# A fused RWKV-6 attention and SwiGLU kernel: all steps of its hand-ordered schedule put into a new order

## The chip, the core and the metric

The kernel runs on one core of a Trainium2 chip. The core has five engines, each with a queue of its own that it works off in order: TensorE (PE in the profile; its weight loads are shown apart as PEld), VectorE (DVE), ScalarE (ACT), GpSimd (POOL) and SyncE (SP), which here only starts transfers. The metric is the device time of one execution in microseconds (us).

## The reference

Attention with a decaying state per head (4 batches, 8 heads, 768 tokens, head dimension 48), and on its output, laid out as 3072 rows of 384, an RMS norm and a SwiGLU feed-forward with 1536 hidden units:

```python
for t in range(S):
    cur = np.einsum('bhd,bhe->bhde', u[None] * kt, vt)
    y[:, :, t] = np.einsum('bhd,bhde->bhe', rt, state + cur)
    state = wt[:, :, :, None] * state + np.einsum('bhd,bhe->bhde', kt, vt)
...
x = np.ascontiguousarray(attn_out.transpose(0, 2, 1, 3)).reshape(B * S, H * D)
xn = x / np.sqrt(np.mean(x * x, axis=-1, keepdims=True) + 1e-06) * rms_g
g = xn @ w_gate
return (g * (1.0 / (1.0 + np.exp(-g))) * (xn @ w_val)) @ w_out
```

## The kernel before

The 768 tokens are cut into six blocks of 128, n = 0 to 5, for each batch j = 0 to 3. Within a block the recurrence is worked out with matrices: the logarithms of w are summed over time by matmuls, r and k are scaled by the exponentials of these sums, their products (masked to the past) give the part within the block, and a state per head carries the rest to the next block. Blocks 0 and 1 of a batch are done together as a pair, with their rows interleaved, so the first steps take 256 tokens of a batch. The four batches of a block make 512 rows for the feed-forward: 12 units of 128 hidden columns for the gate and 12 for the value, then the product with w_out for each 128 rows. The first such group is cut in halves of 256 rows.

The program is a list of some 1010 steps, one string, in which a step is a function name and two numbers. In most names the numbers are block and batch; `gate_mm.3.10` is block 3, unit 10. A loop at the end calls them in that order:

```python
for step in ORDER.split():
    fn, n, j = step.split(".")
    fns[fn](int(n), int(j))
```

Each function issues a handful of instructions, so the string sets the order in which each engine and each DMA queue gets its work; nothing reorders it later. The steps that the text below speaks of:

- `load_r`, `load_k`, `load_v`, `load_w`: 384 KB each on SP's queue into the stage tiles; `load_gv.g.h`: a third of the gate (h = 0, tiles wg_sb0, wg_sb4, wg_sb8) or value weights (h = 1, wv_sb0, 4, 8) on POOL's queue; `load_wo`: a third of w_out, there too.
- `ln` (ACT), `pcs_mm` or `cs_mm` (PE, sums over time), `cs_add` (DVE), `exp_r` and `exp_k` (ACT), `r_mul` (DVE: r times its factor, tile rk), `k_mul` (DVE or POOL).
- `rk_pe` and `rk_tr`: scaled r and k transposed, in the pair by PE and a copy on ACT, later by DMA transposes on SP's queue (tile rkT).
- `pq_mm` (pair) or `q_mm`: products of r and k on PE; `pmask_e`, `pmask_o`: four masks for each batch on DVE (tile qts); `sta_mm`, `sta_cp`: the state halfway through the pair; `st_mm`, `st_new`: the state at the end of a block; `w_tot`: the decay over a whole block.
- `bonus_mul` (POOL, two products, tile ruk), `bonus_sum` (DVE, tile diag), `bonus_v` (POOL, tile ydiag): the term with u; `cast_v`: v to bf16.
- `y_mm` (PE) and `x_add` (DVE, tile xbs): the attention output; `xd_mm`: in place of one x_add, a matmul with an f32 identity that adds ydiag in PSUM.
- `x_sq`, `x_rstd` (on ACT or POOL), `xn_mul`, `xn_pe`, `xn_out` (tile xnt): the norm and its transpose.
- `pgate`, `pval`, `psilu`, `ph` for the first group's halves, `gate_mm`, `val_mm`, `silu`, `h_mul` for the others (tile ht holds the hidden units); `o_mm`, `o_out`, `out_dma`: the last product and the output. `warm`: fillers for PE, two matmuls of zeros.

PSUM has three rings of banks, two for sums and gates, two for sums and values, four for everything else (ps_a, ps_b, ps_q in the names). Which engine does a step in which block is set by short lists of block and batch such as `K_POOL` and `CAST_ACT`.

Of the kernel before, what the change touches and what calls it, by code (L numbers as in the profile page):

```python
# [26 lines left out]
exp_k.1.0 u_mm.0.0 warm.4.2 load_k.0.0 k_mul.1.0 k_mul.0.0 rk_pe.0.0 rk_tr.0.0 u_cp.0.0 bonus_mul.1.0 bonus_sum.1.0
load_v.0.0 load_w.0.2 load_w.0.1 rk_pe.1.0 warm.0.2 warm.1.2 warm.2.2 warm.3.2 warm.6.2 rk_tr.1.0 pq_mm.0.0 cast_v.0.0
pmask_e.0.0 w_tot.0.0 pq_mm.1.0 pmask_e.1.0 bonus_mul.0.0 ln.0.1 pcs_mm.1.1 pcs_mm.2.1 pmask_o.0.0 ln.0.2 sta_mm.0.0
pcs_mm.0.1 exp_r.1.1 exp_k.1.1 load_r.0.1 r_mul.1.1 exp_k.0.1 exp_r.0.1 load_k.0.1 k_mul.0.1 pmask_o.1.0 pcs_mm.0.2  # L30
pcs_mm.1.2 exp_r.1.2 exp_r.0.2 k_mul.1.1 w_tot.0.1 r_mul.0.1 rk_pe.1.1 rk_tr.1.1 w_tot.0.2 sta_cp.0.0 bonus_v.1.0
load_gv.0.0 gain_mm.0.0 rk_pe.0.1 rk_tr.0.1 y_mm.0.0 load_gv.0.1 pcs_mm.2.2 exp_k.1.2 load_v.0.1 gain_cp.0.0
bonus_sum.0.0 pq_mm.1.1 xd_mm.1.0 load_r.0.2 load_w.0.3 r_mul.1.2 r_mul.0.2 bonus_v.0.0 cast_v.0.1 x_add.0.0
pmask_o.1.1 pmask_e.1.1 bonus_mul.0.1 bonus_mul.1.1 pq_mm.0.1 pmask_e.0.1 ln.0.3 pcs_mm.0.3 sta_mm.0.1 warm.5.2
load_gv.2.0 load_k.0.2 k_mul.1.2 load_gv.2.1 bonus_sum.0.1 pmask_o.0.1 bonus_v.0.1 sta_cp.0.1 x_sq.0.0 x_sq.1.0
exp_k.0.2 k_mul.0.2 x_rstd.0.0 xn_mul.1.0 rk_pe.1.2 pcs_mm.1.3 exp_r.0.3 xn_pe.1.0 xn_out.1.0 pcs_mm.2.3 xn_mul.0.0
rk_tr.1.2 y_mm.0.1 bonus_sum.1.1 w_tot.0.3 xn_pe.0.0 xn_out.0.0 exp_r.1.3 exp_k.0.3 exp_k.1.3 load_r.0.3 x_add.0.1
rk_pe.0.2 warm.7.2 rk_tr.0.2 bonus_v.1.1 r_mul.0.3 x_add.1.1 st_mm.0.1 load_k.0.3 pval.1.0 x_sq.0.1 load_gv.1.0
load_gv.1.1 x_sq.1.1 x_rstd.0.1 k_mul.1.3 st_new.0.1 r_mul.1.3 pgate.1.0 k_mul.0.3 bonus_mul.1.3 load_v.0.2 psilu.1.0
pq_mm.1.2 pq_mm.0.2 pmask_e.1.2 pmask_o.0.2 pgate.0.0 pval.0.0 pmask_o.1.2 st_mm.0.0 st_new.0.0 pmask_e.0.2 rk_pe.1.3  # L40
pgate.5.0 xn_mul.0.1 psilu.0.0 ph.0.0 xn_mul.1.1 bonus_mul.0.3 rk_pe.0.3 rk_tr.0.3 psilu.5.0 bonus_mul.0.2 ph.1.0
pgate.4.0 xn_pe.1.1 xn_out.1.1 load_wo.1.0 xn_pe.0.1 xn_out.0.1 rk_tr.1.3 psilu.4.0 pval.5.0 pval.4.0 pgate.1.1 ph.5.0
psilu.1.1 pq_mm.1.3 pq_mm.0.3 pval.0.1 pgate.0.1 psilu.0.1 ph.4.0 pmask_o.0.3 cast_v.0.2 ph.0.1 bonus_sum.0.2
load_wo.2.0 bonus_mul.1.2 load_wo.0.0 bonus_sum.1.3 pgate.3.0 psilu.3.0 pval.1.1 ph.1.1 bonus_v.0.2 load_v.0.3
cast_v.0.3 pgate.2.0 pval.3.0 pgate.2.1 psilu.2.1 pval.2.0 pmask_o.1.3 bonus_sum.0.3 pmask_e.1.3 sta_mm.0.2 sta_cp.0.2
sta_mm.0.3 psilu.2.0 ph.2.0 load_w.2.0 ln.2.1 ph.3.0 bonus_sum.1.2 bonus_v.1.2 pgate.4.1 pmask_e.0.3 sta_cp.0.3 ln.2.0
psilu.4.1 pgate.5.1 psilu.5.1 pval.2.1 y_mm.0.2 x_add.1.2 x_sq.1.2 bonus_v.1.3 x_add.0.2 ph.2.1 y_mm.0.3 x_sq.0.2
x_rstd.0.2 pgate.3.1 psilu.3.1 pval.3.1 xn_mul.1.2 cs_mm.2.0 cs_add.2.0 ph.3.1 exp_r.2.0 bonus_v.0.3 cs_mm.2.1
cs_add.2.1 exp_k.2.1 x_add.0.3 xn_mul.0.2 st_mm.0.2 o_mm.0.1 exp_k.2.0 load_k.2.0 load_r.2.0 k_mul.2.0 load_w.2.2
x_add.1.3 r_mul.2.0 st_new.0.2 x_sq.1.3 exp_r.2.1 w_tot.2.1 x_sq.0.3 x_rstd.0.3 xn_pe.1.2 k_mul.2.1 bonus_mul.2.1  # L50
pval.5.1 o_mm.0.0 o_out.0.0 pval.4.1 xn_pe.0.2 bonus_mul.2.0 xn_mul.1.3 ph.4.1 ph.5.1 w_tot.2.0 o_out.0.1 o_mm.0.3
r_mul.2.1 xn_out.1.2 xn_out.0.2 ln.2.2 cs_mm.2.2 cs_add.2.2 xn_mul.0.3 ln.2.3 out_dma.0.1 load_w.3.0 load_r.2.2
o_out.0.3 exp_r.2.2 xn_pe.0.3 ln.3.0 load_k.2.2 cs_mm.2.3 xn_pe.1.3 rk_tr.2.1 cs_add.2.3 exp_r.2.3 st_mm.0.3 o_mm.0.2
exp_k.2.3 xn_out.0.3 exp_k.2.2 ln.3.1 xn_out.1.3 val_mm.1.5 rk_tr.2.0 w_tot.2.2 k_mul.2.2 r_mul.2.2 bonus_mul.2.2
w_tot.2.3 bonus_sum.2.0 r_mul.2.3 gate_mm.1.5 silu.1.5 h_mul.1.5 gate_mm.1.1 st_new.0.3 o_out.0.2 silu.1.1 out_dma.0.2
val_mm.1.7 k_mul.2.3 load_v.2.0 bonus_sum.2.1 load_v.2.2 bonus_v.2.1 rk_tr.2.2 gate_mm.1.7 silu.1.7 bonus_mul.2.3
cast_v.2.2 h_mul.1.7 bonus_v.2.0 cast_v.2.0 val_mm.1.1 h_mul.1.1 gate_mm.1.2 silu.1.2 gate_mm.1.4 q_mm.2.0 gate_mm.1.3
q_copy_o.2.1 out_dma.0.3 silu.1.4 q_mask_o.2.1 q_copy_o.2.0 q_mask_e.2.0 q_mask_e.2.1 silu.1.3 val_mm.1.2 h_mul.1.2
val_mm.1.6 gate_mm.1.6 cast_v.2.1 q_mask_o.2.0 st_mm.2.2 st_new.2.2 out_dma.0.0 silu.1.6 val_mm.1.4 h_mul.1.4
gate_mm.1.0 rk_tr.2.3 bonus_sum.2.2 q_mm.2.2 q_copy_o.2.2 h_mul.1.6 silu.1.0 gate_mm.1.10 silu.1.10 val_mm.1.0  # L60
y_mm.2.0 q_mask_o.2.2 bonus_v.2.2 h_mul.1.0 load_r.3.0 load_k.3.0 q_copy_o.2.3 q_mask_e.2.2 gate_mm.1.9 silu.1.9
x_add.2.0 x_sq.2.0 bonus_mul.3.1 bonus_sum.2.3 y_mm.2.1 x_add.2.1 x_sq.2.1 q_mask_e.2.3 val_mm.1.9 h_mul.1.9
q_mask_o.2.3 x_rstd.2.0 x_rstd.2.1 val_mm.1.10 gate_mm.1.11 h_mul.1.10 gate_mm.1.8 y_mm.2.2 x_add.2.2 silu.1.8
xn_mul.2.0 xn_mul.2.1 cast_v.2.3 bonus_mul.3.0 val_mm.1.3 h_mul.1.3 load_k.3.2 x_sq.2.2 st_mm.2.0 cs_mm.3.1 st_new.2.0
silu.1.11 val_mm.1.8 load_w.3.2 ln.3.3 h_mul.1.8 y_mm.2.3 val_mm.1.11 h_mul.1.11 xn_pe.2.0 load_v.3.0 cast_v.3.0
cs_mm.3.0 cs_add.3.0 exp_k.3.0 x_rstd.2.2 xn_mul.2.2 cast_v.3.1 bonus_v.2.3 cs_add.3.1 bonus_sum.3.0 bonus_v.3.0
xn_out.2.0 exp_r.3.0 w_tot.3.0 ln.3.2 o_mm.1.0 exp_k.3.1 k_mul.3.1 k_mul.3.0 exp_r.3.1 x_add.2.3 r_mul.3.0 load_r.3.2
o_out.1.0 x_sq.2.3 x_rstd.2.3 o_mm.1.1 w_tot.3.1 cs_mm.3.2 r_mul.3.1 cs_add.3.2 exp_k.3.2 xn_pe.2.1 st_mm.2.3
st_new.2.3 xn_out.2.1 load_w.4.0 load_w.4.2 o_mm.1.2 o_out.1.1 ln.4.0 load_v.3.2 load_v.4.0 bonus_mul.3.3 rk_tr.3.0
cs_mm.3.3 rk_tr.3.1 xn_mul.2.3 ln.4.1 exp_r.3.2 xn_pe.2.2 xn_out.2.2 cs_add.3.3 out_dma.1.0 xn_pe.2.3 r_mul.3.2  # L70
exp_k.3.3 w_tot.3.2 xn_out.2.3 cast_v.4.1 k_mul.3.2 bonus_sum.3.1 o_out.1.2 load_w.5.2 o_mm.1.3 st_mm.2.1 exp_r.3.3
w_tot.3.3 st_mm.3.0 st_new.3.0 r_mul.3.3 rk_tr.3.2 ln.4.2 val_mm.2.0 st_new.2.1 gate_mm.2.3 silu.2.3 k_mul.3.3
rk_tr.3.3 o_out.1.3 load_k.4.2 load_r.4.0 val_mm.2.3 h_mul.2.3 gate_mm.2.1 silu.2.1 bonus_mul.3.2 gate_mm.2.0 silu.2.0
q_mm.3.0 q_mask_e.3.0 q_copy_o.3.0 q_mask_e.3.1 gate_mm.2.7 gate_mm.2.2 silu.2.2 st_mm.3.1 cast_v.3.3 q_mask_o.3.0
bonus_v.3.1 load_r.4.2 h_mul.2.0 y_mm.3.0 silu.2.7 out_dma.1.2 q_copy_o.3.1 q_mask_o.3.1 val_mm.2.7 gate_mm.2.11
val_mm.2.1 x_add.3.0 x_sq.3.0 x_rstd.3.0 out_dma.1.3 st_new.3.1 h_mul.2.7 bonus_sum.3.3 cast_v.4.0 q_mm.3.2
q_copy_o.3.3 h_mul.2.1 q_mask_e.3.3 cast_v.3.2 q_mask_o.3.3 bonus_v.3.3 load_k.5.2 bonus_mul.4.3 silu.2.11 val_mm.2.11
q_mask_e.3.2 gate_mm.2.6 h_mul.2.11 y_mm.3.1 st_mm.3.3 gate_mm.2.5 val_mm.2.2 st_new.3.3 val_mm.2.6 load_k.4.0
h_mul.2.2 q_copy_o.3.2 q_mask_o.3.2 silu.2.5 xn_mul.3.0 st_mm.3.2 load_w.5.0 y_mm.3.3 silu.2.6 x_add.3.1 h_mul.2.6
x_sq.3.1 gate_mm.2.4 silu.2.4 x_add.3.3 x_sq.3.3 bonus_sum.4.3 val_mm.2.10 gate_mm.2.10 silu.2.10 h_mul.2.10  # L80
val_mm.2.5 gate_mm.2.8 x_rstd.3.1 xn_mul.3.1 gate_mm.2.9 h_mul.2.5 load_v.4.2 x_rstd.3.3 xn_mul.3.3 silu.2.8
bonus_sum.3.2 val_mm.2.4 h_mul.2.4 val_mm.2.8 silu.2.9 y_mm.3.2 st_new.3.2 h_mul.2.8 bonus_mul.4.2 xn_pe.3.3 ln.5.0
out_dma.1.1 load_k.5.0 ln.4.3 val_mm.2.9 h_mul.2.9 xn_out.3.3 bonus_mul.4.1 bonus_v.3.2 cs_mm.4.1 cs_mm.4.0 cs_add.4.0
exp_k.4.0 cs_add.4.1 exp_r.4.1 xn_pe.3.0 xn_out.3.0 load_r.5.2 r_mul.4.1 x_add.3.2 exp_k.4.1 k_mul.4.1 exp_r.4.0
# [742 lines left out]
```

## Time and profile before

| | |
|---|---|
| median of 3 executions | 201.58 us (199.26 to 391.27) |
| profiled execution, its own time | 200.24 us |
| its span | 198.5 us |
| PE, PEld busy | 190.4, 122.2 us |
| DVE, ACT, POOL busy | 145.4, 137.8, 122.8 us |
| DMA | 32.44 MB, mean 163 GB/s |
| granted TensorE clock | 1.0 |

The times from the trace are against the span; 1.74 us lie around it. One of the three executions took 391.27 us, the other two are within 1.2% of one another, and the profiled one lies between these. Busy time is a sum of durations, and a matmul's duration in the trace is longer than the time after which the next one starts, so PE at 96% is partly overlap.

### The profile page before, as it was taken

The numbers are of one execution on the slowest core, as the hardware profiler recorded it, in microseconds if no ns is written. First come the engines' busy times: TensorE is split into PE (matmuls) and PEld (weight loads), VectorE is DVE, ScalarE is ACT, GpSimd is POOL, SyncE is SP. The second block draws the span as 40 slices with busy tenths as digits, with TensorE's granted clock in tenths as the row PEclk, the third lists the DMA queues.
The fourth block names the chain that finished last, engine by engine and source line by source line (L and its number), as shares of the span: only waits on it lengthen the run. The fifth ranks groups of instructions, "written<-read, shape, count | busy, mean of one in ns | idle before, by whom it ended". The sixth has DMA issues, their size and how long they took to land.

```text
span 198.5 us, 5008 instructions
## 1 busy us (share of the span) xinstructions
PE 190.4 (96%) x1932; PEld 122.2 (62%) x1948; DVE 145.4 (73%) x291; ACT 137.8 (69%) x274; POOL 122.8 (62%) x168
## 2 busy tenths in 40 slices
...
PEclk9999999999999999999999999999999999999999
...
GB/s 167 325 323 235 258 221 207 229 214 178 209 146 226 245 202 226 221 210 196 243 207 215 244 146 145 43 40 99 140 122 133 2 25 139 40 0 40 122 59 99
DMA packets 109377, 32.44 MB, mean 163 GB/s; under 512 B 103461, under 2 KB 108969, under 8 KB 109353
## 3 DMA queue, kind: packets, MB, share of 16 engines
...
q0 software_dynamic: 2832, 3.54, 10.2%
...
q14 instruction: 10, 0.07, 0.1%
...
## 4 chain that ended last, share of the span: by engine, by line
PE 65%; DMA 14%; POOL 7%; DVE 6%; SPq 4%; issue 2%; ACT 1%; DVEq 0%; POOLq 0%
PE ps_bu L712 9%; PE ps_au L712 8%; PE ps_av L712 8%; PE ps_qx L769 7%; PE ps_bv L712 7%; DMA wv_sb<-in_moe_w_val_dram 5%; PE ps_qu L769 5%; SPq L259 4%; DMA stage_r<-in_r_dram 3%; DMA stage_v<-in_v_dram 3%; PE ps_qz L769 3%; PE ps_qv L769 3%; DMA stage_w<-in_w_dram 2%; POOL ruk L494 2%; POOL ruk L493 2%
## 5 line engine op out<-in xcount | busy, mean ns | idle before, releaser
L769 PEld LDWEIGHTS <-ht 128*128 128x128 bf16 x300 | 28.4, 98 | 17.0 <-DVE ht L755 0.4
L235 ACT ACTIVATE sg<-ps_au 128x512 bf16<-128x512 f32 x36 | 21.5, 597 | 14.1 <-PE ps_au L712 11.1
L755 DVE TENSOR_TENSOR ht<-ps_bu,sg 128x512 bf16<-128x512 f32 x31 | 21.3, 686 | 12.5 <-ACT sg L235 6.2
L712 PEld LDWEIGHTS <-wv_sb 128*128 128x128 bf16 x180 | 19.4, 114 | 16.9 <-issue 1.6
L235 ACT ACTIVATE sg<-ps_av 128x512 bf16<-128x512 f32 x36 | 21.5, 597 | 11.9 <-PE ps_av L712 8.4
L712 PEld LDWEIGHTS <-wg_sb 128*128 128x128 bf16 x180 | 19.1, 114 | 16.6 <-DVE rk L481 0.8
L493 POOL TENSOR_TENSOR ruk<-stage_r,stage_k 128x384 f32<-128x384 f32 x24 | 24.0, 1000 | 7.0 <-DMA stage_r<-in_r_dram 3.7
L487 POOL TENSOR_TENSOR rk<-stage_k,ek 128x384 bf16<-128x384 f32 x20 | 19.9, 1004 | 10.4 <-ACT ek L235 6.4
L712 PE MATMUL ps_bu<-xnt,wv_sb 128*128 128x512 bf16 x88 | 24.6, 379 | 1.2 <-DVE ht L755 0.8
L494 POOL TENSOR_TENSOR ruk<-ruk,u_bc 128x384 f32<-128x384 f32 x24 | 23.9, 998 | 1.9
L712 PE MATMUL ps_av<-xnt,wg_sb 128*128 128x512 bf16 x89 | 24.9, 380 | 0.2
L755 DVE TENSOR_TENSOR ht<-ps_bv,sg 128x512 bf16<-128x512 f32 x29 | 19.9, 685 | 6.7 <-ACT sg L235 3.0
L712 PE MATMUL ps_au<-xnt,wg_sb 128*128 128x512 bf16 x85 | 23.5, 381 | 0.3
L712 PE MATMUL ps_bv<-xnt,wv_sb 128*128 128x512 bf16 x82 | 23.0, 380 | 0.2
L503 POOL TENSOR_TENSOR ydiag<-stage_v,diag 128x384 f32<-128x384 f32 x24 | 19.7, 830 | 4.5 <-DVE diag L498 4.3
L668 POOL TENSOR_TENSOR rstd<-rstd,mhalf 128x1 f32<-128x1 f32 (+1 forms) x18 | 10.0, 561 | 12.4 <-ACT junk L654 12.4
L769 PE MATMUL ps_qu<-wo_sb,ht 128*128 128x384 bf16 x96 | 16.9, 326 | 0.0
L233 ACT ACT_TABLE_LOAD x12 | 15.4, 1283 | 1.9 <-PEq L811 1.7
L654 ACT ACTIVATE junk<-xbs 128x385 bf16<-128x385 f32 (+1 forms) x23 | 12.2, 529 | 5.8 <-DVE xbs L637 5.7
L672 ACT ACTIVATE xn<-xbs,rstd 128x384 bf16<-128x384 f32 x23 | 13.6, 608 | 3.2 <-POOL rstd L668 3.2
L498 DVE TENSOR_REDUCE diag<-ruk 128x8 f32<-128x384 f32 x24 | 13.0, 544 | 3.7 <-POOL ruk L494 3.7
L769 PE MATMUL ps_qx<-wo_sb,ht 128*128 128x384 bf16 (+1 forms) x96 | 15.0, 306 | 0.0
...
## 6 DMA issues: line engine op xcount, KB each, us to landing
stage_w<-in_w_dram SPq DMA_DIRECT2D x12, 384.0 KB, 5.6
stage_r<-in_r_dram SPq DMA_DIRECT2D x12, 384.0 KB, 6.3
stage_k<-in_k_dram SPq DMA_DIRECT2D x12, 384.0 KB, 6.0
stage_v<-in_v_dram SPq DMA_DIRECT2D x12, 384.0 KB, 5.2
...
wg_sb<-in_moe_w_gate_dram POOLq DMA_DIRECT2D x3, 384.0 KB, 8.0
wv_sb<-in_moe_w_val_dram POOLq DMA_DIRECT2D x3, 384.0 KB, 9.8
```

The costliest lines, as they stand in the source:

```text
L233: nc.scalar.preload_act_table_set(table_name)
L235: return nc.scalar.activation(**kw).ins
L487: eng.tensor_tensor(out=rk[:, n % 2, j, 1, :, 0:D], in0=inp["k", n, j], in1=bank["ek", n, j][:, 0:DM].rearrange("p (h d) -> p h d", h=H), ...
L493: nc.gpsimd.tensor_tensor(out=ruk[n, j], in0=inp["r", n, j], in1=inp["k", n, j], op=ALU.mult)
L494: nc.gpsimd.tensor_tensor(out=ruk[n, j], in0=ruk[n, j], in1=u_bc, op=ALU.mult)
L498: nc.vector.tensor_reduce(out=diag[n, j].rearrange("p h o -> p (h o)"), in_=ruk[n, j], axis=mybir.AxisListType.X, op=ALU.add)
L503: nc.gpsimd.tensor_tensor(out=ydiag[n, j], in0=inp["v", n, j], in1=diag[n, j].to_broadcast([128, H, D]), op=ALU.mult)
L654: nc.scalar.activation(out=junk[:, 0:DM + own], in_=xbuf[n, j] if own else xb[n, j], func=AF.Square, accum_out=rstd[key][:, 0, i:i + 1])
L672: nc.scalar.activation(out=xn, in_=xb[n, j], func=AF.Copy, scale=rstd[0, j][:, 1, n:n + 1] if n in PAIR else rstd[n, j][:, 1, 0:1])
L712: nc.tensor.matmul(ps, lhsT=units(ws, c, f), rhs=xnt[n][:, c, :], start=(c == 0), stop=(c == KC - 1))
L755: nc.vector.tensor_tensor(out=ht[n][:, f, :], in0=bank.pop(("v", n, f)), in1=bank.pop(("sg", n, f)), op=ALU.mult)
L769: nc.tensor.matmul(ps[:, cols], lhsT=ht[n][:, f, b * L:(b + 1) * L], rhs=wo_sb[:, f, cols], start=(f == 0), stop=(f == FC - 1))
```

## The change

The string is new from its start to `y_mm.4.3 gate_mm.3.0`, some seven tenths of it; the rest is as before. With it go these changes in who does what:

- `xd_mm.1.0` is gone; `x_add.1.0` on DVE takes its place, and the f32 identity is no longer made.
- `pcs_mm.2.2`, an addition on DVE before, is two matmuls as in the other batches.
- `cast_v` of batches 1 and 2 goes from ACT to POOL, that of batch 0 from POOL to ACT.
- `k_mul` of 0.0, 0.3 and 1.3 goes from POOL to DVE, that of 0.2 from DVE to POOL (with K_POOL go the buffers of `exp_k`).
- `x_rstd.0.1` goes from ACT to POOL.
- One filler step fewer (seven); the causal mask mask_le has a tile of its own rather than a part of xbs.

New branches in `pq_mm`, `pmask` and `y_mm`, for batches whose pair is not cut in halves, are not taken: every batch has a `sta_mm` step and so is in SPLIT.

```diff
 ORDER = """
-load_w.0.0 ln.0.0 pcs_mm.1.0 exp_r.1.0 exp_k.0.0 load_r.0.0 r_mul.1.0 pcs_mm.0.0 exp_r.0.0 r_mul.0.0 pcs_mm.2.0
...
+load_w.0.0 ln.0.0 pcs_mm.1.0 pcs_mm.2.0 exp_k.1.0 load_k.0.0 k_mul.1.0 u_mm.0.0 exp_r.1.0 exp_k.0.0 u_cp.0.0
...
-    CAST_ACT = sel("01 02 03")
+    CAST_ACT = sel("00 03")
-    K_POOL = sel("00 03 11 13 20 21 22 23 30 31 32 33 40 41 42 43 50 51 52 53")
+    K_POOL = sel("02 11 20 21 22 23 30 31 32 33 40 41 42 43 50 51 52 53")
-    X_PE = sel("10")
+    X_PE = sel("")
-    PCS_ADD = sel("22")
+    PCS_ADD = sel("")
+    ODD_COPY = sel("")
-    RSTD_ACT = sel("00 01")
+    RSTD_ACT = sel("00")
+    SPLIT = {int(x.split(".")[2]) for x in ORDER.split() if x.startswith("sta_mm")}
...
-    mask_le = xbs[:, 2, 0:64].bitcast(BF16)
+    mask_le = const.tile([128, 128], BF16)
...
-    ident_f = const.tile([128, 128], FP32)
-    nc.gpsimd.tensor_copy(out=ident_f, in_=ident)
+    if X_PE:
+        ident_f = const.tile([128, 128], FP32)
+        nc.gpsimd.tensor_copy(out=ident_f, in_=ident)
```

DVE in the front, before: from the sum for the bonus of batch 1 (diag) to the state halfway through the pair of batch 1 (st, sta_cp), which y_mm.0.1 reads. rk rows are r_mul and k_mul, qts rows masks, xbs rows x_add.

```order
L498 TENSOR_REDUCE diag_472<-ruk_291 128x8
L481 TENSOR_TENSOR rk_150<-stage_r_72,ps_bu_356 128x8x48
L481 TENSOR_TENSOR rk_150<-stage_r_72,ps_av_342 128x8x48
L637 TENSOR_TENSOR xbs_80<-ps_qu_392,ydiag_498 128x384
L549 TENSOR_TENSOR qts_492<-ps_qv_475,mask_q_76 128x512
L549 TENSOR_TENSOR qts_492<-ps_qx_474,mask_q_76 128x512
L549 TENSOR_TENSOR qts_529<-ps_qu_511,mask_q_76 128x512
L487 TENSOR_TENSOR rk_150<-stage_k_73,ps_au_467 128x8x48
L498 TENSOR_REDUCE diag_567<-ruk_505 128x8
L549 TENSOR_TENSOR qts_529<-ps_qv_512,mask_q_76 128x512
L568 TENSOR_TENSOR st_153<-ps_qx_543,half_of_138 128x384
```

The same engine and place in the change:

```order
L480 TENSOR_TENSOR wcol_493<-ps_av_340,half_of_139 128x8
L485 TENSOR_TENSOR rk_151<-stage_r_72,ps_av_340 128x8x48
L485 TENSOR_TENSOR rk_151<-stage_r_72,ps_bv_358 128x8x48
L663 TENSOR_TENSOR xbs_80<-ps_qv_418,ydiag_330 128x384
L663 TENSOR_TENSOR xbs_80<-ps_qx_419,ydiag_332 128x384
L587 TENSOR_TENSOR st_154<-ps_qv_525,half_of_139 128x384
L491 TENSOR_TENSOR rk_151<-stage_k_73,ps_au_354 128x8x48
L502 TENSOR_REDUCE diag_555<-ruk_360 128x8
L561 TENSOR_TENSOR qts_514<-ps_qz_497,mask_q_76 128x512
L561 TENSOR_TENSOR qts_587<-ps_qx_569,mask_q_76 128x512
L561 TENSOR_TENSOR qts_587<-ps_qv_570,mask_q_76 128x512
L561 TENSOR_TENSOR qts_514<-ps_qu_496,mask_q_76 128x512
```

The two r_mul of batch 2 (stage_r) stay ahead of the masks of batch 1. All four of these masks now come last, behind sta_cp.0.1, and two x_add rather than one stand ahead of them; st_new.0.0, which came later before, stands just ahead of the first row shown.

POOL's queue where it issues the weights, before:

```order
L371 DMA wg_sb8_161<-in_moe_w_gate_dram 128x3x512
L371 DMA wv_sb8_164<-in_moe_w_val_dram 128x3x512
L503 TENSOR_TENSOR ydiag_570<-stage_v_74,diag_567 128x384
L503 TENSOR_TENSOR ydiag_712<-stage_v_74,diag_682 128x384
L371 DMA wg_sb4_160<-in_moe_w_gate_dram 128x3x512
L371 DMA wv_sb4_163<-in_moe_w_val_dram 128x3x512
```

and in the change:

```order
L375 DMA wg_sb4_159<-in_moe_w_gate_dram 128x3x512
L375 DMA wv_sb4_162<-in_moe_w_val_dram 128x3x512
L507 TENSOR_TENSOR ydiag_713<-stage_v_74,diag_711 128x384
L497 TENSOR_TENSOR ruk_747<-stage_r_72,stage_k_73 128x384
L498 TENSOR_TENSOR ruk_747<-ruk_747,u_bc_77 128x384
L694 TENSOR_TENSOR rstd_756<-rstd_756,mhalf_145 128x2
L375 DMA wg_sb8_160<-in_moe_w_gate_dram 128x3x512
L417 CAST vp_838<-stage_v_74 128x768
L381 DMA wo_sb_157<-in_moe_w_out_dram 128x1536
L497 TENSOR_TENSOR ruk_868<-stage_r_72,stage_k_73 128x384
L498 TENSOR_TENSOR ruk_868<-ruk_868,u_bc_77 128x384
L375 DMA wv_sb8_163<-in_moe_w_val_dram 128x3x512
```

The middle third (tiles with 4) now comes ahead of the last (with 8), and the last pair is split: its gate part stands behind x_rstd.0.1 (rstd), its value part behind a cast, a load of w_out and a bonus product.

SP's queue in the middle, where r of block 4, batches 2 and 3, is loaded (`load_r.4.2`). Before it is one of the two in the third row; rkT rows are the transposes of block 3:

```order
L518 DMA_TRANSPOSE rkT_2016<-rk_150 128x8x128 x2
L259 DMA stage_k_73<-in_k_dram 128x16x48
L259 DMA stage_r_72<-in_r_dram 128x16x48 x2
L259 DMA stage_k_73<-in_k_dram 128x16x48 x2
L259 DMA stage_w_75<-in_w_dram 128x16x48
```

In the change it is the first load of stage_r, ahead of the transposes of batches 2 and 3:

```order
L522 DMA_TRANSPOSE rkT_1893<-rk_151 128x8x128 x2
L262 DMA stage_r_72<-in_r_dram 128x16x48
L522 DMA_TRANSPOSE rkT_2020<-rk_151 128x8x128 x2
L262 DMA stage_v_74<-in_v_dram 128x16x48
L262 DMA stage_k_73<-in_k_dram 128x16x48
```

`load_r.4.2` is thus issued one pair of transposes earlier; `load_r.4.0` follows later.

188 lines of the change are left out of this document (105 added, 83 removed).

## The prediction

> **What bounds the kernel now.** I read four views in this order: the page's busy line, the table of windows, the timelines around the first 60 us, and the chain of waits. The page and the windows first; in a window's row the columns are its length, then the busy time of PE, PE's weight loads, DVE, ACT and POOL, then clock, DMA share and GB/s.
>
> ```profile
> PE 190.4 (96%) x1932; PEld 122.2 (62%) x1948; DVE 145.4 (73%) x291; ACT 137.8 (69%) x274; POOL 122.8 (62%) x168
> PEclk9999999999999999999999999999999999999999
> ```
>
> ```profile
> 0.00:10.00 10.00, 8.64 (x56) 4.63 (x56) 4.83 (x22) 5.59 (x8) 6.12 (x20) 1.00 0.90 246
> 10.00:20.00 10.00, 9.09 (x227) 6.63 (x226) 9.64 (x22) 9.48 (x20) 9.42 (x11) 1.00 1.14 278
> 20.00:30.00 10.00, 9.63 (x188) 8.15 (x189) 9.04 (x19) 9.34 (x21) 9.80 (x13) 1.00 1.20 239
> ...
> 100.00:110.00 10.00, 9.13 (x80) 5.50 (x80) 7.87 (x16) 7.16 (x15) 7.51 (x10) 1.00 1.15 212
> ...
> 190.00:198.50 8.50, 5.26 (x41) 3.48 (x38) 2.29 (x5) 0.00 (x0) 0.00 (x0) 1.00 0.26 93
> sum 198.50, PE 190.41 PEld 122.22 DVE 145.44 ACT 137.82 POOL 122.83; mean PE 9.52 PEld 6.11 DVE 7.27 ACT 6.89 POOL 6.14
> ```
>
> TensorE sets the time. It is without work for 198.50 - 190.41 = 8.1 us: 1.36 in the first window and 3.24 in the last, which hold the first load and the last output, and 3.5 in the 180 us between. A matmul's duration in the trace is longer than its place in the queue, so I price TensorE by start to start. In the chain of waits three matmuls of 512 columns follow one another every 0.65 us, which is their price:
>
> ```profile
> 59.59 0.65 PE ps_av L712 x3
> 60.24 0.65 PE ps_au L712 x3
> ```
>
> So a new order can gain what TensorE waits (3.5 us in all) and what work is taken off it, and it can lose without such a bound. The idle lies in two places: 10 to 30 us, where DVE, ACT and POOL are each busy for over nine tenths and TensorE is fed by them (0.91 + 0.37), and 100 to 110 us (0.87).
>
> **The change, part by part. Work on TensorE.** The identity matmul of batch 0's second block (xd_mm.1.0) goes, two f32 matmuls that hold the queue from 17.44 to 18.28, or 0.84 us; DVE's x_add of 0.47 replaces it. pcs_mm.2.2 becomes two bf16 matmuls, and one filler step of two matmuls goes; both have this form, 0.33 for two (8.74 to 9.07):
>
> ```profile
> 17.44 0.91 PE L641 MATMUL ps_qz<-ydiag,ident_f 128*128 128x384 f32 x2
> 18.28 0.24 PE L544 MATMUL ps_qu<-rkT 48*64 48x128 bf16 x1
> ...
> 8.74 0.49 PE L271 MATMUL ps_bu<-still 128*128 128x384 bf16 x2
> 9.07 0.49 PE L271 MATMUL ps_bv<-still 128*128 128x384 bf16 x2
> ```
>
> In sum -0.84 + 0.33 - 0.33 = -0.84 us of TensorE work. It counts only from the point where TensorE, not DVE, sets the pace. I take y_mm.0.1 as that point (the second batch's attention product): before it DVE decides, behind it TensorE runs through its queue.
>
> **When y_mm.0.1 can start.** Before, the mask products on DVE begin at 10.61 and y_mm.0.1 starts at 21.89, just behind the end of DVE's st at 21.73:
>
> ```profile
> 10.61 0.69 DVE L549 TENSOR_TENSOR qts<-ps_qz,mask_q 128x512 bf16<-128x512 f32 x1 [0.31 <-PE ps_qz L544]
> 11.22 0.15 DVE L476 TENSOR_TENSOR wcol<-ps_au,half_of 128x8 f32<-128x8 f32 x1
> 11.29 0.68 DVE L549 TENSOR_TENSOR qts<-ps_qu,mask_q 128x512 bf16<-128x512 f32 x1
> 11.89 0.68 DVE L549 TENSOR_TENSOR qts<-ps_qv,mask_q 128x512 bf16<-128x512 f32 x1
> ...
> 16.32 0.56 DVE L481 TENSOR_TENSOR rk<-stage_r,ps_bu 128x384 bf16<-128x384 f32 x1
> 16.79 0.55 DVE L481 TENSOR_TENSOR rk<-stage_r,ps_av 128x384 bf16<-128x384 f32 x1
> ...
> 21.18 0.55 DVE L568 TENSOR_TENSOR st<-ps_qx,half_of 128x384 bf16<-128x384 f32 x1
> ```
>
> ```profile
> 21.89 0.23 PE L615 MATMUL ps_qx<-st,rkT 128*64 128x96 bf16 x1
> ```
>
> A mask costs DVE 0.60 (11.29 to 11.89), an operation of 384 columns 0.47 (16.32 to 16.79), a small one 0.07 (11.22 to 11.29). In the change the first mask waits for rk_pe.0.0, its copy on ACT and pq_mm.0.0; I walk these with before's spacings to 11.24, 0.6 later. From there DVE has eight masks, twelve operations of 384 columns and three small ones until the last mask that y_mm.0.1 needs: seven masks to that one's start 4.2, 12 x 0.465 = 5.6, 0.2, then the mask itself 0.68 and 0.16 to the matmul, together 10.8, so 22.1 if nothing waits.
>
> One thing does. r_mul.0.2 stands 4.9 us into this stretch (four masks, five operations, three small ones), at 16.2, and reads r of batch 2, now the eleventh load of the queue. Before, the eleventh is issued at 11.48, and the four loads of r in the first 20 us have a median of 6.2 us to landing, those of w 4.8:
>
> ```profile
> 11.48 1.15 SPq L259 DMA_DIRECT2D stage_w<-in_w_dram  x1
> ...
> stage_w<-in_w_dram SPq DMA_DIRECT2D x4, 384.0 KB, 4.8
> stage_r<-in_r_dram SPq DMA_DIRECT2D x4, 384.0 KB, 6.2
> ```
>
> That gives 16.3 to 17.7. I take 17.4, near the late end, since a weight transfer starts at 14.9 and shares the engines. DVE loses 1.2 and y_mm.0.1 starts at 23.3, **+1.4** against 21.89. Bounds: +0.3 with the early landing (a wait of 0.1), +1.7 with the late one, and +0.2 if the first mask also came at 10.61 (DVE is then at r_mul.0.2 at 15.6 and waits 0.7 for a load of 16.3).
>
> What waits behind the masks is less by four steps, which the new order puts ahead of y_mm.0.1, where TensorE has spare time: xn_pe.0.0 (three matmuls of 128 columns, 31.12 to 31.29 below, 0.16), rk_pe.0.2 (eight of that width, by the same row 0.45), st_mm.0.0 (28.14 to 28.48, 0.34) and a filler that is gone (0.33): **-1.27**. The matmul that is gone stood ahead of y_mm.0.1 and is thus not counted again.
>
> ```profile
> 28.14 0.50 PE L587 MATMUL ps_qx<-vp,rk 128*128 128x96 bf16 x8
> 28.48 0.61 PE L510 MATMUL ps_qv<-ident,rk 128*128 128x128 bf16 x8
> 29.33 0.41 PE L719 MATMUL ps_au<-xnt,wg_sb 128*128 128x256 bf16 x2 [0.24 <-DMA wg_sb<-in_moe_w_gate_dram]
> 31.12 0.33 PE L684 MATMUL ps_qx<-ident,xn 128*128 128x128 bf16 x3
> 31.29 0.33 PE L684 MATMUL ps_qz<-ident,xn 128*128 128x128 bf16 x3
> 31.92 0.41 PE L719 MATMUL ps_bv<-xnt,wv_sb 128*128 128x256 bf16 x2 [0.31 <-DMA wv_sb<-in_moe_w_val_dram]
> ```
>
> **The rest of the front and the weights.** These rows show before's two stalls there: 29.33 - 28.48 less the 0.45 of that rk_pe step, so 0.4, and 31.92 - 31.29 less 0.16, so 0.47; both for weights. In the change both waits go elsewhere. DVE is still late for rk_pe.0.3 (r_mul.0.3, 0.8), pgate.2.1 (0.2) and rk_pe.1.3: together 1.0 against 0.89, **+0.1**.
>
> The weights come in another order, from POOL's queue: the second pair (wg4, wv4) is issued at about 21, where before it was 24.4, but wg8 stands behind x_rstd.0.1 and wv8 behind a cast, a w_out load and two more products: I place them at 28.8 and 32.8, against 21.3 and 22.05 before.
>
> ```profile
> 24.41 0.80 POOL L371 DMA_DIRECT2D wg_sb<-in_moe_w_gate_dram  x1
> ...
> 22.05 9.82 DMA wv_sb<-in_moe_w_val_dram
> ...
> DMA to landing us min/median/max: 6.3/8.0/10.2
> ...
> DMA to landing us min/median/max: 8.6/9.8/11.8
> ```
>
> (The last two lines are those of the wg_sb and the wv_sb tile.) wg8 is needed by pgate.5.0 at about 35.5 and lands at 28.8 + 6.3 to 10.2 = 35.1 to 39.0; wv8 is needed by pval.5.1 at 40.0 and lands at 32.8 + 8.6 to 11.8 = 41.4 to 44.6 by these rows, or at 39.1 with the 6.3 of the least loaded transfer. So 0 to 4.6 us of stall. By then the load queue wants little (the input of the first two blocks has been issued), so I lean to the short end: **+0.5**, with both ends kept.
> [...]
>
> **The middle.** Before, the load of r.4.2 holds up a chain into TensorE:
>
> ```profile
> 95.63 6.50 DMA stage_r<-in_r_dram
> ```
>
> ```profile
> 102.26 1.00 POOL L493 TENSOR_TENSOR ruk<-stage_r,stage_k 128x384 f32<-128x384 f32 x1 [3.69 <-DMA stage_r<-in_r_dram]
> 104.37 0.55 DVE L498 TENSOR_REDUCE diag<-ruk 128x8 f32<-128x384 f32 x1 [2.10 <-POOL ruk L494]
> 103.94 0.81 PE L712 MATMUL ps_au<-xnt,wg_sb 128*128 128x512 bf16 x3
> 105.57 0.81 PE L712 MATMUL ps_bu<-xnt,wv_sb 128*128 128x512 bf16 x3 [0.82 <-DVE ht L755]
> ```
>
> POOL is idle 3.69 for the load, DVE 2.10 for POOL's product, and the ht multiply queued behind DVE's reduction is late: 105.57 - 103.94 - 0.65 = 0.98 of TensorE. In the change load_r.4.2 stands ahead of the transposes rk_tr.3.2 and 3.3 on SP, and bonus_sum.4.3 behind the last ht multiply of that block. That stall goes, and the small ones at 87 to 98 with it (0.5 by start to start): -1.5 at best. But a chain on POOL and DVE is tighter: x_rstd.3.2, k_mul.4.0, bonus_mul.4.0, bonus_sum.4.0, then xn_out.3.2 and 3.3, which gate_mm.3.10 needs; I walk it to 0.5 behind TensorE. Bounds -1.5 to +0.5, or as bad as POOL's old wait, +3.7. I take **-0.7**.
>
> From y_mm.4.3 on nothing changes. ACT loads two tables fewer, under TensorE's work, at no gain.
>
> **The sum** against the profiled execution (span 198.5, its time 200.24, which is 0.7% under the median of 201.58): +1.4 - 1.27 + 0.1 + 0.5 - 0.7 = 0.0. I forecast **200.3 us**, span 198.5, no change. Two per cent, 4.0 us, is about what a measurement of this kernel can tell from none.
>
> **The rivals.** (A) *Weights late, slower.* If wv8 takes its 11.8 us, pval.5.1 waits from 40.0 to 44.6: 200.3 - 0.5 + 4.6 = 204.4. It decides when the last weight lands later than 44. For it: the last transfer of each kind was the slowest before, and wv8 is issued 10.8 us later. Against it: before, the loads of two blocks ran beside them. 0.15.
> (B) *POOL's chain in the middle late, slower.* If x_rstd.3.2 or the transposes hold bonus_mul.4.0 for as long as before's 3.69, no gate matmul stands ready to cover it: 200.3 + 0.7 + 3.7 = 204.7 at most, 204 likely. For it: POOL is the engine with the longest queue of one-microsecond work. Against it: ten gate and val steps of the block before stand ahead. 0.07.
> (C) *The front is not late, faster.* If the first mask comes at 10.6 and r.2 lands at 16.3, no wait of the front is left behind y_mm.0.1, all weights are in time and the middle runs without a stall: +1.4 becomes +0.2, +0.1 becomes -0.9, +0.5 becomes 0 and -0.7 becomes -1.5: 0.2 - 1.27 - 0.9 - 1.5 = -3.5, so 196.8. For it: the bounds above. Against it: four walks must all come out at their good ends, and before's own 3.5 us of idle between the first and the last window leaves little beyond. 0.12.
> (D) *The clock.* Now the granted clock is full in all 40 slices, the first ones under the fillers at the start. With one filler step fewer and waits of at most 0.9 us in my walk, nothing should change; were the clock halved over five microseconds of the front, it would cost about 2.5, so 202.8. 0.02. [...]
>
> **How the numbers follow.** The forecast has 0.64, its own range 198.3 to 203.5 (weights and middle at their usual ends). Faster by over 2% (under 196.2) is a third of C and the forecast's edge: 0.07. Slower (over 204.2) is over half of A and B and 0.09 of the forecast's, whose walks carry errors that add: 0.23. The rest, 0.70, lies within. The range is 197.0 to 206.0: below it lies half of C, above it a late weight with another wait on top.
>
> **What would show it.** Right: in the new trace y_mm.0.1 starts at 23 to 23.5 with DVE idle about 1.2 before an r_mul for stage_r; xd_mm's f32 matmuls are gone; POOL's idle for stage_r near 100 us is under 1, and the 100 to 110 window of TensorE is above 9.6; the matmuls that read wv8 first wait under 1 us, and bonus_sum.4.0 keeps gate_mm.3.10 waiting under 1 us. Wrong: TensorE idle of over 2 us in one piece anywhere, a releaser of wv_sb or wg_sb in the 30 to 45 window, y_mm.0.1 before 22, or a span outside 195.3 to 204.3.

## Result: 0.6% faster, no change by 2%, and the profile after

The changed kernel's median is 199.39 us (20 executions) against 200.82 for the one before (20): ratio 0.9942, 95% interval 0.9925 to 0.9958, or 1.2 us faster. The profiled execution takes 199.57 us with a span of 197.9 (before 200.24 and 198.5). The forecast was 200.3, no change, with a range of 197.0 to 206.0. Executions well above the fastest of the same kernel (391 and 280 us here, 201.8 to 209.8 us in the experiments) are left out of the ratios, and the spans of two of them out of the table of experiments.

The page's busy line and the windows after, with the columns as before:

```profile
PE 190.9 (96%) x1930; PEld 122.3 (62%) x1946; DVE 146.9 (74%) x293; ACT 134.7 (68%) x269; POOL 122.1 (62%) x167
```

```profile
10.00:20.00 10.00, 9.13 (x218) 6.64 (x216) 7.84 (x18) 9.11 (x17) 9.76 (x12) 1.00 1.09 276
20.00:30.00 10.00, 9.39 (x189) 7.43 (x188) 9.97 (x21) 9.81 (x21) 7.46 (x10) 1.00 1.20 243
...
100.00:110.00 10.00, 9.87 (x95) 6.15 (x95) 9.48 (x18) 7.95 (x18) 9.43 (x14) 1.00 1.06 199
...
sum 197.90, PE 190.88 PEld 122.34 DVE 146.87 ACT 134.69 POOL 122.10; mean PE 9.54 PEld 6.12 DVE 7.34 ACT 6.73 POOL 6.11
```

TensorE's idle fell from 8.1 to 7.0 us. It rose from 20 to 30 us (0.37 to 0.61) and all but went in the middle (100 to 110 us: 0.87 to 0.13). Of both sums some 0.8 us is no idle: the page's lines count 16 matmuls fewer than weight loads (1932 and 1948 before, 1930 and 1946 after), because 16 records of matmuls of 512 columns are missing from these two traces, and each missing one leaves a gap of 0.05.

Where the time went, by the starts of the same steps in the two traces (each wait is an excess, start to start against the price of the same work; the 1.27 of the second row is the prediction's own price of the four steps, so it is no separate measurement):

| stretch of TensorE's queue | before | after | difference | forecast |
|---|---|---|---|---|
| start of y_mm.0.1 | 21.89 | 24.38 | +2.5 | +1.4 |
| work left behind it | 168.06 | 166.79 | -1.27 | -1.27 |
| waits from there to 60 us | 1.96 | 1.59 | -0.37 | +0.6 (front 0.1, weights 0.5) |
| waits from 60 to 128 us | 2.37 | 1.12 | -1.25 | -0.7 |
| waits behind, in unchanged order | 0.96 | 0.72 | -0.24 | 0 |
| sum | | | -0.6 | 0.0 |

The front, on DVE and TensorE:

```profile
11.88 0.69 DVE L561 TENSOR_TENSOR qts<-ps_qu,mask_q 128x512 bf16<-128x512 f32 x1
...
17.11 0.15 DVE L480 TENSOR_TENSOR wcol<-ps_av,half_of 128x8 f32<-128x8 f32 x1
17.91 0.56 DVE L485 TENSOR_TENSOR rk<-stage_r,ps_av 128x384 bf16<-128x384 f32 x1 [0.65 <-DMA stage_r<-in_r_dram]
...
23.11 0.68 DVE L561 TENSOR_TENSOR qts<-ps_qu,mask_q 128x512 bf16<-128x512 f32 x1
23.71 0.55 DVE L723 TENSOR_TENSOR xnt<-ps_qx,gT 128x384 bf16<-128x384 bf16 x1
```

```profile
24.38 0.23 PE L641 MATMUL ps_qx<-st,rkT 128*64 128x96 bf16 x1
```

The first mask starts at 11.88 (walked: 11.24). r of batch 2 is waited for, as forecast, though for 0.73 by the spacing (17.18 to 17.91) and not 1.2. The last mask starts at 23.11, and y_mm.0.1 not 0.84 behind it but 1.27. Between them stands rk_pe.0.2, which the new order puts ahead of y_mm.0.1 on TensorE and which writes the bank that the last mask reads out:

```profile
23.85 0.61 PE L514 MATMUL ps_qu<-ident,rk 128*128 128x128 bf16 x8 [0.27 <-DVE qts L561]
```

It starts as the mask ends (23.79) and has a price of 0.45, so y_mm.0.1 could not start before 24.3. The bank that y_mm.0.1 itself writes, ps_qx, is read out by DVE's xn_out (the xnt row) until 24.26, which is nearly as late and costs 0.1 at most.

The weights, and TensorE where it first reads the last pair:

```profile
29.64 0.83 POOL L375 DMA_DIRECT2D wg_sb<-in_moe_w_gate_dram  x1
...
33.88 0.81 POOL L375 DMA_DIRECT2D wv_sb<-in_moe_w_val_dram  x1
...
DMA to landing us min/median/max: 7.4/7.9/9.9
```

```profile
36.78 0.85 PE L745 MATMUL ps_av<-xnt,wg_sb 128*128 128x256 bf16 x6
...
41.39 0.71 PE L745 MATMUL ps_bv<-xnt,wv_sb 128*128 128x256 bf16 x5
```

(The third line is the wv_sb tile's.) wv8 was issued at 33.88 and took 7.4, so it landed at 41.3, 0.1 before its first matmul. wg8, issued at 29.64, took 7.1 and landed 0.05 before its own. Neither row has a wait.

### The profile page after: what moved, and what is told of

The parts are those of the page before. It is cut to its first block, busy times and chain, and to the rows that moved or that the text cites. A ratio compares the mean times of both kernels' runs of the same rounds, so it can differ in the third digit from the quotient of the medians.

```text
span 197.9 us, 5024 instructions
## 1 busy us (share of the span) xinstructions
PE 190.9 (96%) x1930; PEld 122.3 (62%) x1946; DVE 146.9 (74%) x293; ACT 134.7 (68%) x269; POOL 122.1 (62%) x167
## 4 chain that ended last, share of the span: by engine, by line
PE 84%; SPq 5%; DVE 5%; DMA 3%; issue 1%; DVEq 0%
PE ps_av L738 10%; PE ps_bu L738 10%; PE ps_au L738 10%; PE ps_bv L738 9%; PE ps_qz L795 6%; PE ps_qx L795 6%; SPq L262 5%; PE ps_qv L795 5%; PE ps_qu L795 5%; DMA stage_r<-in_r_dram 3%; PE ps_au L745 3%; PE ps_bv L745 2%; PE ps_bu L745 2%; PE ps_av L745 2%; DVE xnt L727 2%
## 5 line engine op out<-in xcount | busy, mean ns | idle before, releaser
L238 ACT ACTIVATE sg<-ps_au 128x512 bf16<-128x512 f32 x36 | 21.4, 595 | 14.9 <-PE ps_au L738 13.2
L781 DVE TENSOR_TENSOR ht<-ps_bu,sg 128x512 bf16<-128x512 f32 x30 | 20.6, 686 | 12.7 <-ACT sg L238 6.8
L781 DVE TENSOR_TENSOR ht<-ps_bv,sg 128x512 bf16<-128x512 f32 x30 | 20.6, 686 | 9.1 <-PE ps_bv L738 4.7
L738 PE MATMUL ps_bu<-xnt,wv_sb 128*128 128x512 bf16 x86 | 24.0, 380 | 0.2
L694 POOL TENSOR_TENSOR rstd<-rstd,mhalf 128x1 f32<-128x1 f32 (+1 forms) x19 | 10.8, 570 | 21.7 <-ACT junk L680 21.4
L738 PE MATMUL ps_bv<-xnt,wv_sb 128*128 128x512 bf16 x86 | 23.6, 379 | 0.3 <-issue 0.2
L491 POOL TENSOR_TENSOR rk<-stage_k,ek 128x384 bf16<-128x384 f32 x18 | 17.9, 1003 | 2.7 <-ACT ek L238 2.6
L698 ACT ACTIVATE xn<-xbs,rstd 128x384 bf16<-128x384 f32 x24 | 14.1, 609 | 2.3 <-POOL rstd L694 2.2
L598 POOL TENSOR_SCALAR_AFFINE_SELECT qts<-qts 128x512 bf16<-128x512 bf16 x16 | 10.0, 635 | 7.7 <-ACT qts L595 7.7
L795 PE MATMUL ps_qz<-wo_sb,ht 128*128 128x384 bf16 (+1 forms) x84 | 12.9, 303 | 0.0
```

Of the source, the lines that this page charges most:

```text
L238: return nc.scalar.activation(**kw).ins
L491: eng.tensor_tensor(out=rk[:, n % 2, j, 1, :, 0:D], in0=inp["k", n, j], in1=bank["ek", n, j][:, 0:DM].rearrange("p (h d) -> p h d", h=H), ...
L698: nc.scalar.activation(out=xn, in_=xb[n, j], func=AF.Copy, scale=rstd[0, j][:, 1, n:n + 1] if n in PAIR else rstd[n, j][:, 1, 0:1])
L738: nc.tensor.matmul(ps, lhsT=units(ws, c, f), rhs=xnt[n][:, c, :], start=(c == 0), stop=(c == KC - 1))
L781: nc.vector.tensor_tensor(out=ht[n][:, f, :], in0=bank.pop(("v", n, f)), in1=bank.pop(("sg", n, f)), op=ALU.mult)
L795: nc.tensor.matmul(ps[:, cols], lhsT=ht[n][:, f, b * L:(b + 1) * L], rhs=wo_sb[:, f, cols], start=(f == 0), stop=(f == FC - 1))
```

## The experiments

All times are against the kernel before on the same chip, as ratios with a 95% interval; a profile is one execution.

| what runs | ratio | interval | span |
|---|---|---|---|
| the change | 0.9942 | 0.9925 to 0.9958 | 197.9 |
| old front, new middle | 0.9922 | 0.9884 to 0.9959 | 196.7 |
| new front, old middle | 0.9957 | 0.9929 to 0.9984 | - |
| before, r's load early | 1.0017 | 0.9980 to 1.0054 | 198.3 |
| before, sum late | 0.9979 | 0.9941 to 1.0017 | 199.0 |
| before, weights 2 us early | 1.0156 | 1.0056 to 1.0257 | 201.0 |
| the change, wv8 4 us late | 1.0084 | 1.0035 to 1.0134 | 200.6 |
| before, no identity matmul | 0.9984 | 0.9949 to 1.0018 | 198.8 |
| old front, weights early, new middle | 1.0121 | 1.0043 to 1.0199 | - |
| old front without identity matmul, new middle | 0.9916 | 0.9889 to 0.9943 | 197.4 |
| the change, r early | 0.9934 | 0.9903 to 0.9966 | 197.3 |
| the change, r and wv8 early | 0.9933 | 0.9901 to 0.9965 | 197.6 |
| before again | 0.9991 | 0.9953 to 1.0029 | 199.4 |

**Which half gains.** The list was cut between the first and the second feed-forward group, and the halves were crossed.

```diff
- (old list) ... exp_k.2.2 ln.3.1 xn_out.1.3 val_mm.1.5 rk_tr.2.0 ... (old list)
+ (old list) ... exp_k.2.2 ln.3.1 xn_out.1.3 (new list without the steps already done)
```

> The old order (and the old lists of engines) up to the first unit of the second group, val_mm.1.5, and from there the new order. Theory (the new front loses 0.47 us at TensorE's 60th us, the new middle gains 1.25): 1.2 to 1.5 us faster than before, and some 0.5 us faster than the whole change. Rival (the middle's gain hangs on the times that the new front hands over): within 0.3 us of before, with a wait of 0.3 us or more on TensorE between 60 and 128 us that the whole change does not have.

Its span is 196.7, 1.8 less than before's, and the ratio 0.9922. Between 60 and 130 us it has less idle, as the change has (before, this, the change):

```profile
60.00:100.00 40.00, 39.56 (x351) 23.42 (x355) 34.64 (x67) 30.69 (x63) 33.73 (x47) 1.00 1.15 223
100.00:130.00 30.00, 28.97 (x261) 17.48 (x264) 24.67 (x50) 22.49 (x48) 24.75 (x31) 1.00 0.83 162
```

```profile
60.00:100.00 40.00, 39.60 (x343) 23.56 (x347) 33.39 (x66) 30.83 (x64) 31.40 (x44) 1.00 1.04 214
100.00:130.00 30.00, 29.74 (x275) 18.28 (x278) 27.12 (x54) 23.89 (x51) 26.96 (x35) 1.00 0.87 161
```

```profile
60.00:100.00 40.00, 39.56 (x338) 23.49 (x343) 32.79 (x64) 30.82 (x63) 31.73 (x43) 1.00 1.04 212
100.00:130.00 30.00, 29.71 (x278) 18.28 (x281) 26.96 (x54) 23.73 (x52) 27.62 (x37) 1.00 0.85 160
```

By these windows the gain is in the last stretch (28.97 to 29.74 busy of 30). A sharper measure is the time from the start of the first matmul of the second group to that of the last matmul of all, since behind that point each of these versions has the same 197 steps of TensorE to do:

| profile | second group starts | from there to the last matmul |
|---|---|---|
| before, two profiles | 58.78, 59.53 | 136.24, 136.35 |
| before, r's load early; sum late | 58.49, 58.53 | 136.26, 136.96 |
| before, no identity matmul; weights early | 58.91, 60.35 | 136.33, 137.16 |
| old front, new middle | 58.59 | 134.58 |
| old front without identity matmul, new middle | 59.30 | 134.58 |
| the change | 59.60 | 134.76 |
| the change, r early; r and wv8 early | 58.90, 59.21 | 134.92, 134.85 |
| the change, wv8 late | 62.30 | 134.77 |

Behind the old front the new middle is 1.7 to 2.6 us shorter than the old one in every profile, and behind the new front it is as short: the theory of the middle holds.

> The counterpart: the new order and lists up to val_mm.1.10, and from there the old order. Theory: 0.5 us slower than before (TensorE at its 60th us 0.47 later), with the old wait of about 1 us ahead of val_mm.2.9 back. Rival (the front is where the gain is): 0.5 us or more faster than before.

Here the theory missed. The new front with the old middle is not 0.5 us slower but 0.9 faster (0.9957). Its one profile is of an execution of 205.68 us, in which the second group starts at 65.37, so it can only give a hint. In it the old middle takes 135.08 rather than 136.2 or more, and POOL's wait for r's load is short enough that TensorE does not wait at all between 100 and 116 us:

```profile
106.96 1.00 POOL L498 TENSOR_TENSOR ruk<-stage_r,stage_k 128x384 f32<-128x384 f32 x1 [1.68 <-DMA stage_r<-in_r_dram]
```

If the other executions are like it there, the old middle loses its wait behind the new front too, and the two halves do not add; the medians fit that (behind the new front the new middle gains 0.3 us, 0.9957 to 0.9942, behind the old one 1.6), but no other profile shows it.

By medians the new front is between 0.9 us better (this run) and level (the change against the old front with the new middle, 0.9942 and 0.9922, with intervals that overlap); by single profiles it is worse: at the start of the second group the change stands at 59.60, before at 58.78 and, in the second profile below, at 59.53. What sets median and profile apart is how far executions differ. Those of the change lie between 199.1 and 200.3, those of the new front with the old middle between 199.5 and 200.4; those of before on that chip between 199.6 and 202.0, of the old front with the new middle between 198.4 and 200.6. The old front is at times the faster one and varies more. The kernel before was profiled once more to see why:

> The kernel before, unchanged, for a second look at where its executions differ. If the weights are what varies: its waits at rk_pe.1.3 and xn_pe.0.1 differ by 0.2 us or more from 0.41 and 0.48. If r's load at 95 us is: the wait at gate_mm.2.9 differs from 0.98 as much. Ratio 1.000 within its interval.

```profile
24.61 0.21 PE L620 MATMUL ps_qx<-vp,qts 64*64 64x48 bf16 x1 [0.82 <-issue]
```

```profile
106.44 0.81 PE L712 MATMUL ps_bu<-xnt,wv_sb 128*128 128x512 bf16 x3 [0.95 <-DVE ht L755]
```

In this execution (201.08 us, span 199.4) the two weights were not waited for; instead y_mm.0.1 started 0.54 later (22.43), and TensorE stood 0.82 inside it for nothing that the profile shows. So the weights alone are not what varies in the old front, and its cause stays open. The middle's wait (the second row; the step is val_mm.2.4, by the order of the string, where the expectations name gate_mm.2.9 and val_mm.2.9) varies too, and the profile that the forecast was made from had the smallest of it: the idle ahead of that row is 0.82 there, 0.95 here, 1.18 and 1.61 in the experiments without the identity matmul and with early weights. That is part of the median gain that the two profiles (0.67 apart) don't show.

**The middle's wait: the load or the place of the sum.** Each was done alone in the kernel before.

```diff
-load_w.5.2 rk_tr.3.2 rk_tr.3.3 load_k.4.2 load_r.4.0 load_r.4.2      (SP)
+load_w.5.2 load_r.4.2 rk_tr.3.2 rk_tr.3.3 load_k.4.2 load_r.4.0
```

> The kernel before with one step moved: load_r.4.2 ahead of rk_tr.3.2 on SP. Theory A (the late load is the cause of the wait at 104 us): POOL's idle of 3.69 us ahead of bonus_mul.4.3 under 0.5, and 0.9 to 1.0 us faster. Theory B (the place of bonus_sum.4.3 on DVE is the cause): no change. Theory C: the load's issue of 2.4 us holds up the transposes rk_tr.3.2 and 3.3 behind it, and as much is lost at q_mm.3.2: no change or 1 us slower.

```profile
96.78 0.23 PE L531 MATMUL ps_qv<-rkT 48*128 48x128 bf16 x1 [0.89 <-DMA rkT<-rk]
```

```profile
88.22 1.36 SPq L259 DMA_DIRECT2D stage_r<-in_r_dram  x1
89.75 4.25 SPq L518 DMA_TRANSPOSE rkT<-rk  x2
```

Theory C: POOL no longer waits for r, the wait at val_mm.2.4 is gone, and TensorE waits 0.89 at an earlier step, q_mm.3.2, for the transposes that the load now stands ahead of on SP. No gain (1.0017). The change puts the load at the same place, but orders other work between these transposes and q_mm.3.2.

```diff
-bonus_sum.4.3 val_mm.2.10 ... gate_mm.2.9 h_mul.2.5      (DVE)
+val_mm.2.10 ... gate_mm.2.9 h_mul.2.5 bonus_sum.4.3
```

> The kernel before with one step moved: bonus_sum.4.3 behind h_mul.2.5 on DVE, so that the two ht products no longer stand behind it. Theory A (the late load is the cause): POOL still idles 3.7 us, its masks and rstd steps come late, y_mm.3.2 or xn_pe.3.3 waits instead, and at most 0.3 us is gained. Theory B (the place on DVE is the cause): TensorE's wait of 0.98 us goes, 0.9 to 1.0 us faster, though POOL idles as before.

```profile
107.15 0.34 PE L684 MATMUL ps_qz<-ident,xn 128*128 128x128 bf16 x3 [0.98 <-ACT xn L672]
```

```profile
102.75 1.00 POOL L493 TENSOR_TENSOR ruk<-stage_r,stage_k 128x384 f32<-128x384 f32 x1 [4.43 <-DMA stage_r<-in_r_dram]
```

Theory A: POOL still idles (4.43), its rstd step behind the product is late, and TensorE waits 0.98 for xn instead. The time is the same within its interval (0.9979). In both profiles the wait only moves to the next queue. That the gain needs the load, the sum and the gap ahead of q_mm.3.2 together is inferred: the new middle has all three, and no run has just these.

**The weights.** On POOL, in the change, wv8 was put behind two more products; in the kernel before, wg8 and wv8 were put ahead of one.

```diff
-load_gv.2.1 bonus_mul.0.3 bonus_mul.1.3      (the change)
+bonus_mul.0.3 bonus_mul.1.3 load_gv.2.1
```

> The changed kernel with load_gv.2.1 (wv8) behind two more bonus products on POOL, issued about 4 us later (37.8). It landed at 41.30 and was needed at 41.39. If nothing but this weight gates pval.5.1, TensorE waits 3.5 to 4.0 us there and the time rises by as much, to about 203 (the mechanism of rival A, at its price). If the queue is less loaded by then, it lands after 5 us rather than 7.4 and the wait is 1.5. If there were slack elsewhere, under 1 us.

```profile
37.10 0.85 PE L745 MATMUL ps_av<-xnt,wg_sb 128*128 128x256 bf16 x6 [0.50 <-DMA wg_sb<-in_moe_w_gate_dram]
44.05 0.85 PE L745 MATMUL ps_bv<-xnt,wv_sb 128*128 128x256 bf16 x6 [2.17 <-DMA wv_sb<-in_moe_w_val_dram]
```

The wait is 2.17, not 3.5 to 4, since wv8 took 6.3 us to land here and 7.4 in the change; why it was quicker is not shown. The time rises by 1.4% of before's over the change, 2.8 us, and the span by 2.7, which is the sum of the two waits shown: rival A's mechanism is real and nothing hides it. wg8, which was not moved, is waited for 0.50 in this execution and not at all in the change's, where it landed 0.05 ahead: it has no margin to speak of.

```diff
-bonus_mul.1.1 load_gv.2.0 load_gv.2.1      (before)
+load_gv.2.0 load_gv.2.1 bonus_mul.1.1
```

> The kernel before with two steps moved on POOL: load_gv.2.0 and 2.1 ahead of bonus_mul.1.1, so that wg8 and wv8 are issued 2 us earlier (about 19.3 and 20.1). Theory W (TensorE waits at rk_pe.1.3 and xn_pe.0.1 for these two weights, and their landing is what differs between executions of the old front): both waits, 0.41 and 0.48, under 0.15, 0.6 to 0.9 us faster, and undisturbed executions within 1.0 us of one another where those of before spread over 2.4. Rival (the engines are full, so that an earlier weight only delays a load of r or k): another wait of as much ahead of 35 us, no change in time or spread.

> The old front with its two weights 2 us earlier (as in the experiment on the weights) and the new middle. Theory W: the gains add, 0.6 to 0.9 us faster than the old front with the new middle alone, about 2.2 us faster than before and 1 us faster than the whole change. Rival: no better than the old front with the new middle alone (1.6 us faster than before).

Both fell the other way: 1.6% and 1.2% slower than before, though the wait for wv8 goes; the ratios rest on two and three executions, so their sizes are rough. In the first one wg8 and wv8 are issued at 19.72 and 20.52, 1.5 us earlier than before, and POOL's k_mul of batch 3 starts at 29.51 (26.01 before) after an idle of 3 us:

```profile
29.51 0.99 POOL L487 TENSOR_TENSOR rk<-stage_k,ek 128x384 bf16<-128x384 f32 x1 [3.03 <-ACT sg L235]
```

The ACT instruction that the view names gives nothing that k_mul reads; of what it reads, ek was written at 24.4, which leaves stage_k. That load is issued at 16.2 in all three profiles at hand, and takes 13.2 us to land here (at 29.4), against 9.4 and 11.7 in the two profiles of before. TensorE then waits 1.4 at rk_pe.1.3. That the weights took k's share of the DMA engines is inferred from this, not shown.

**The new front's waits.** In the change, r of batch 2 was loaded earlier, and DVE's sum of batch 1 put behind the masks.

```diff
-load_v.0.0 load_v.0.1 load_w.0.3 load_r.0.2      (SP)
+load_v.0.0 load_w.0.3 load_r.0.2 load_v.0.1
-bonus_mul.0.1 load_gv.0.1 ... bonus_v.0.1 load_gv.1.0 load_gv.1.1      (POOL)
+load_gv.0.1 bonus_mul.0.1 ... load_gv.1.0 load_gv.1.1 bonus_v.0.1
-bonus_sum.0.1 pmask_o.1.1 pmask_e.0.1 pmask_o.0.1 pmask_e.1.1      (DVE; the four masks keep their order)
+pmask_o.1.1 pmask_e.0.1 pmask_o.0.1 pmask_e.1.1 bonus_sum.0.1
```

> The changed kernel with what holds its front up moved: load_w.0.3 and load_r.0.2 ahead of load_v.0.1 on SP; bonus_sum.0.1 behind the four masks of batch 1 on DVE; on POOL load_gv.0.1 ahead of bonus_mul.0.1 and load_gv.1.0 and 1.1 ahead of bonus_v.0.1. DVE's wait for r (0.65) goes and y_mm.0.1 starts at 23.2 to 23.7 in place of 24.38. Theory 1 (the late front is lost time): 0.7 to 1.2 us faster than the change. Theory 2 (its weights land 0.05 to 0.7 us before they are needed, so an earlier front runs into them): waits for wg_sb or wv_sb at pgate.2.0, pgate.5.0 or pval.5.1 that take back 0.5 us or more; within 0.3 us of the change.

```profile
23.54 0.20 PE L641 MATMUL ps_qx<-st,rkT 128*64 128x96 bf16 x1 [0.32 <-DVE xnt L723]
```

r is no longer waited for, y_mm.0.1 starts at 23.54, and the row shows what holds it now: DVE's xn_out, which frees its bank. No wait for a weight appears: wv8 is issued 0.76 earlier here (33.12), so POOL moved with the front, and theory 2's mechanism is not there. The span is 0.6 less than the change's, the medians (199.43 and 199.39) are level. Between the theories this is inconclusive: a profile is one execution, and the ratio 0.9934 lies within the interval of the change's.

> The same, and load_gv.2.1 (wv8) right behind load_gv.2.0, some 3.4 us earlier. Theory 2: the wait at pval.5.1 goes, that at pgate.5.0 for wg8 stays; 0.5 us faster than the same without it. Rival (an earlier weight pushes back the loads of block 2): a wait of 0.3 us or more for k or r of block 2 between 40 and 60 us, no faster.

0.9933: nothing further, and no wait for k or r of block 2 either. Since the run before had no weight wait to remove, it tells nothing new.

**The identity matmul.**

```diff
-pq_mm.1.1 xd_mm.1.0 ... bonus_v.0.0 cast_v.0.1 x_add.0.0
+pq_mm.1.1 ... bonus_v.0.0 cast_v.0.1 x_add.1.0 x_add.0.0
```

> The kernel before with xd_mm.1.0 replaced by x_add.1.0 on DVE, just ahead of x_add.0.0 (mask_le in a tile of its own, no f32 identity). Theory (DVE sets the pace ahead of y_mm.0.1, so TensorE work taken off there counts nothing): TensorE 0.84 us less work, y_mm.0.1 0.2 to 0.5 us later than 21.89, time 0.0 to 0.5 us slower. Rival (the matmul's 0.84 us counts): y_mm.0.1 earlier and 0.5 to 0.84 us faster.

```profile
22.93 0.23 PE L613 MATMUL ps_qu<-st,rkT 128*64 128x96 bf16 x1
```

TensorE has 0.84 less to do, y_mm.0.1 starts no earlier, and the time is the same (0.9984). That speaks for the theory, that work taken off TensorE where DVE sets the pace counts nothing; but the interval reaches down to 0.9949 and so does not exclude the rival's 0.5 to 0.84 us. The size of the delay, 1.0 against the first profile of before (22.93 and 21.89), cannot be put down to the one DVE operation: the unchanged kernel's second profile has 22.43, and here TensorE's granted clock was at half just ahead of that point:

```profile
15.30:18.70 3.40, 2.37 (x105) 2.07 (x104) 3.26 (x9) 3.33 (x6) 3.17 (x5) 1.00 1.11 232
18.70:22.10 3.40, 3.40 (x52) 2.48 (x44) 3.40 (x7) 3.30 (x10) 3.32 (x4) 0.50 1.20 229
```

The next experiment has the same front, and its profile has the full clock there; y_mm.0.1 starts at 22.31 in it, 0.42 later than in the first profile of before, as expected.

> The old front without the identity matmul (x_add.1.0 on DVE, as in the experiment on it), and the new middle from val_mm.1.5 on. If the two add, as they do where TensorE runs through its queue: 1.2 to 1.9 us faster than before, as the old front with the new middle was, and executions within 1.5 us of one another. Rival (the two do not add): within 0.5 us of before.

0.9916, with executions from 198.1 to 199.8: 198.59 us median. It is the fastest version by its median and ratio, ahead of the change by 0.3% of before's time, and its interval and that of the change still overlap. TensorE is busy without a gap from 60 to 130 us (the 39.60 and 29.74 of the old front with the new middle above are not worse: that trace, like before's and the change's, misses 16 records of matmuls, and this one misses none):

```profile
60.00:100.00 40.00, 40.00 (x345) 23.48 (x345) 33.38 (x66) 31.03 (x63) 31.47 (x43) 1.00 1.03 214
100.00:130.00 30.00, 30.00 (x283) 18.39 (x282) 27.14 (x55) 23.72 (x51) 27.70 (x37) 1.00 0.86 156
```

## Why the prediction was right, step by step

- **What bounds the kernel**: right. TensorE set the time, and what an order could gain was its idle and the work taken off it; the span fell by 0.6 and the median by 1.2. The 3.5 us of idle was some 0.8 too high, for the missing records. So were the small stalls at 87 to 98 us, put at 0.5: the rows at 87.90 and 93.97 show two matmuls in place of three, and only the 0.27 ahead of 89.90 is a wait.
- **y_mm.0.1 at 23.3**: right in kind, 1.1 short. The first mask came 0.64 later than walked, the wait for r was 0.5 shorter, DVE had small gaps of 0.5, and rk_pe.0.2, which the walk left out between the last mask and y_mm.0.1 though it had counted it as moved ahead, cost 0.43, with the bank that xn_out frees nearly as late.
- **Work on TensorE**: right as far as it is shown. Without the identity matmul y_mm.0.1 does not start earlier in either profile, and no gain in time is seen, though one of 0.5 us is not excluded.
- **Weights, +0.5 of 0 to 4.6**: 0 was measured. wv8 came 1.1 later than placed and took 7.4 rather than up to 11.8. The front was 1.1 later as well, but it is not what saved it: with r early, y_mm.0.1 and wv8's issue both come 0.8 earlier, and there is still no wait. The mechanism at its lower size is in the run with wv8 late (2.17).
- **Rest of the front, +0.1**: with the weights, -0.37 in place of +0.6. The 1.0 us for which DVE was to be late behind y_mm.0.1 did not come: from there to 60 us no row of TensorE shows a wait in the change.
- **The middle, -0.7 of -1.5 to +0.5**: -1.25, and near the good end: the tighter chain on POOL cost nothing that the trace shows. The reason given (load and sum) was only half of it; each alone gives nothing that the runs show, and behind the new front the old middle may lose little of its wait.
- **Nothing changes from y_mm.4.3 on**: 0.24 of waits went there in an unchanged order. That is of the size in which executions differ and was not followed up.

The errors, +1.1, -1.0, -0.55 and -0.24, cancel down to -0.6: that the total came so close is luck, its parts are off by up to 1.1 us. Rival A did not come, though the two last weights landed 0.1 and 0.05 us ahead of their first matmuls. B did not come: POOL's longest idle between 88 and 118 us is 1.73. C's good middle came without its good front. D did not come in the change: the granted clock stayed at 0.96 or above in every window.
